# A fused attention and feed-forward block on one core: head loads and products by halves, late score and output folds in one batch

## The chip, the cores and the metric

The kernel runs on one core of one Trainium2 chip. A core has a matrix engine (TensorE, PE in the profile), a vector engine (VectorE, DVE), an activation engine (ScalarE, ACT), GpSimd (POOL), a queue engine for transfers (SyncE, SP) and 16 DMA engines. On-chip memory is SBUF, with 128 partitions; TensorE writes to PSUM. The metric is device time in microseconds.

## The reference

With x of 2048 tokens and 512 channels in bfloat16, and six vectors of 512 taken from a condition vector c:

```python
mod = (silu(c) @ w_mod).reshape(1, 6, 1, -1)      # sa, ca, ga, sb, cb, gb
h = layernorm(x) * (1 + ca) + sa
q, k, v = split(h @ wqkv)                          # 32 heads of 16 channels
logits = q . k[pos - 2*w] * 16**-0.5               # w = 0..7, positions below 0 masked
x = x + ga * ((softmax(logits) . v[pos - 2*w]) @ wo)
h = layernorm(x) * (1 + cb) + sb
x = x + gb * ((gelu(h @ w_gate) * (h @ w_up)) @ w_down)     # inner width 1792
```

So each token attends to eight tokens at distances 0, 2, ... 14.

## The kernel before

Tokens are cut into five groups, of 256, 256, 512, 512 and 512 (`GROUPS`). Each group passes through: the first layer norm and its shift and scale (`ln1`, then `transposed`, giving `hT`, channels on partitions), q, k and v (`emit_qkv`), attention and its projection (`emit_attention`), the second norm (giving `h2T`), and the feed-forward part (`emit_ffn`).

The head of the program: x's first 256 tokens are loaded, then `wm01`, the two blocks of w_mod that give sa and ca, then wq and wk. `mod_first` turns wm01 and silu(c) into columns with matrix products of one column (`modT_ps`): first for channel block 0, then for blocks 1 to 3. For group 0 VectorE applies shift and scale straight from PSUM (L561); `mod_keep` copies them to SBUF for the other groups, where ScalarE applies them (L519). The variance becomes 1/sqrt by a power on GpSimd (L513). Matmuls without use (`warm_ps`, L430) fill TensorE's time until the first data.

Attention works without gathers on k: VectorE multiplies q by shifted views of k, into product tiles `pq` of 128x2048 (L691). TensorE sums their channels with a 0/1 matrix of 32 columns, four such matmuls at once in four column groups (`LT`, L701: "fold"). For a 512-token group there are eight product tiles; two times four are made, and each four is folded by its own batch of 16 matmuls. Softmax runs over `LT` (`Lb`, `e`, `ss`). v goes through DRAM: `vT` is written to `scr`, and read back shifted as `vR`, four transfers of 32 partitions each for a tile (L667). VectorE forms `pv` = e times vR (L766, L772), TensorE folds these into `o_ps` (L782), also in two batches for a 512-token group, ScalarE copies them to `oT` (L788), and TensorE projects with wo (`x_ps`, L806).

The feed-forward part makes, for each 128-column unit of 1792, `g_ps` and `u_ps` (L847); ScalarE takes gelu and a copy (L856, L859), VectorE multiplies them into `hht` (L860), and TensorE forms `y_ps` (L873); VectorE adds it to x (L881), which is stored. gb is not applied at the end: `mod_row` makes gb as a row (`mb_ps`, L501, from the two halves of `wm5`), and VectorE scales w_down with it once (WdP, L901, seven instructions). ga is applied to wo in the same way, from wm2.

The order of everything is set ahead by a planner (`Plan.order`): each operation has an engine, an assumed duration, what it reads and writes, and a priority from the table `PRI`; the planner places them one after another, and each engine then runs its list in that order. Nearly all transfers are issued by SP in its planned order, and each issue can wait for the data it reads or the buffer that it overwrites.

Of the kernel before, what the change touches and what calls it, by code (L numbers as in the profile page):

```python
# [184 lines left out]
class Engines:  # L185
    def __init__(self, nc, pl):
        op = pl.op
        self.pe = lambda us, fn, **kw: op("pe", us, fn, **kw)
        self.act = lambda us, fn, **kw: op("act", us, fn, **kw)
        self.dve = lambda us, fn, **kw: op("dve", us, fn, **kw)  # L190
        self.pool = lambda us, fn, **kw: op("pool", us, fn, **kw)
        self.dma = lambda n, fn, bw=350e3, us=0.5, **kw: op("sp", us, fn, dma=n / bw, **kw)

# [5 lines left out]
BLOCKS2 = ()  # L199
PRI = {  # L200
        "ln1": (-1549, -553.9, -424.8, -117.9, 420.6),
        "qkv": (-226.2, 479.5, 310.9, 823.2, 1490.9),
        "att": (-63.2, 258.1, -1202.2, 1315.4, 916.4),
        "ffn": (1214.3, 2234.3, 2417.5, 2391, 546),
        "glu": (-1006.6, 100.6, -1510.2, -71.4, 1415.7),
        "mod": (393, -373, -33.5),
        "wo": 1028.5,
        "wd": 1181.4,
        "scr": -3561.5,
        "vR": -3846.6,  # L210
        "warm": (12, 4, 0, 3),
        "load": {"wv": -989.49, "x1": -989.99, "x2": -962.38, "wm2": -989.49, "wo": -888.99, "x3": -991.49,
        "wm3": -899.52, "wm4": -990.99, "x4": -981.04, "Wg": -864.95, "Wu": -877.79, "wm5": -867.98, "Wd":
        -873.85},
}
Plan.MARGIN = {"pe": 0.34, "act": 1.25, "dve": 0.46, "pool": -1.19, "sp": 1.04}
Plan.AHEAD = 2.79
Plan.SKEW = 1.27
# [4 lines left out]
def kernel(  # L223
# [40 lines left out]
    pool("trs", 8, space=bass.MemoryType.DRAM)  # L264
# [18 lines left out]
    onecol = ctile([P, 1], BF16, "onecol")  # L283
    M = ctile([P, H], BF16, "Mph")
# [24 lines left out]
    def consts_dve():  # L309
        nc.vector.memset(warm(), 0.0)  # L310
        nc.vector.memset(one1[:], 1.0)
        nc.vector.memset(neghalf[:], -0.5)
        nc.vector.memset(onecol[:], 1.0)

# [29 lines left out]
    dve(0.6, consts_dve, w=[(early, 0), one1, neghalf, onecol], pri=-1000)  # L344
# [26 lines left out]
    wm01 = T("vR", [P, 4, 2 * D], BF16, "wm01", "early")  # L371
# [21 lines left out]
    def load_rows(t, src, p, cuts, late=0.0):  # L393
        n = len(t.shape) and t.shape[1] // cuts
        for i in range(cuts):
            dma(1835e3 / cuts, lambda i=i: nc.sync.dma_start(
                out=t[:, i * n:(i + 1) * n, :],
                in_=src[i * n * P:(i + 1) * n * P, :].rearrange("(dt p) f -> p dt f", p=P)),
                w=[(t, k) for k in range(i * n, (i + 1) * n)], pri=p + 0.1 * i, bw=385e3)
# [3 lines left out]
    dma(1049e3, lambda: nc.sync.dma_start(out=wm01[:], in_=w_mod[:, 0:2 * D].rearrange("(t p) n -> p t n", p=P)),  # L403
        w=[wm01], pri=-999, bw=385e3)
    for b in range(3):
        dma(524e3, lambda b=b: nc.sync.dma_start(  # L406
            out=wqkv[b][:], in_=A_wqkv[:, b * D:(b + 1) * D].rearrange("(dt p) n -> p dt n", p=P)), w=[wqkv[b]],
            pri=(-998, -997, L["wv"])[b])
# [12 lines left out]
    load_rows(Wg, B_w_gate, L["Wg"], 2)  # L421
    load_rows(Wu, B_w_up, L["Wu"], 2)
    load_wm_halves(wm5, 5, L["wm5"])
    load_rows(WdP, B_w_down, L["Wd"], 2)
# [44 lines left out]
    def mod_first(src, p):  # L469
        parts = []  # L470
        for chs in ((0,), (1, 2, 3)):
            n = len(chs)
            mps = T("psF", [P, 2 * n], F32, "modT_ps")

            def cols(chs=chs, n=n, mps=mps):
                for half in range(2):
                    for i, ch in enumerate(chs):
                        col = mps[:, half * n + i:half * n + i + 1]
                        for kt in range(4):
                            nc.tensor.matmul(col, lhsT=src[:, kt, half * D + ch * P:half * D + (ch + 1) * P],  # L480
# [4 lines left out]
            pe(0.25 * n, cols, r=[src, scT, ident, onecol], w=[mps], pri=p)  # L485
# [3 lines left out]
    def mod_keep(parts, p):  # L489
        for lo, n, mps in parts:  # L490
            act(0.2, lambda lo=lo, n=n, mps=mps: nc.scalar.copy(out=scl[:, lo:lo + n], in_=mps[:, n:2 * n]), r=[mps],
                w=[(scl, 0)], pri=p)
            act(0.2, lambda lo=lo, n=n, mps=mps: nc.scalar.copy(out=modT[:, lo:lo + n], in_=mps[:, 0:n]), r=[mps],
# [13 lines left out]
    def norm(tok, xn, i, mean, rstd, p):  # L507
        dve(0.325, lambda: nc.vector.tensor_scalar(
            out=xn[:, i, :], in0=xrow(tok), scalar1=mean[:, i:i + 1], scalar2=rstd[:, i:i + 1], op0=ALU.subtract,
            op1=ALU.mult), r=[xkey(tok), mean, rstd], w=[(xn, i)], pri=p)  # L510
# [5 lines left out]
    tp0 = []  # L516

    def modulate(dst, src, dt, off, n, p, ins):
        act(act_us(n, 2), lambda: nc.scalar.activation(  # L519
            out=dst[:, dt, 0:n], in_=src(), func=ACT.Identity, scale=scl[:, off // 2 + dt:off // 2 + dt + 1],  # L520
            bias=modT[:, off + dt:off + dt + 1]), r=ins + [(scl, off), (modT, off)], w=[(dst, dt)], pri=p)

    def transposed_by_blocks(xns, dst, off, p):
        blk = T("blk" if off == 0 else "wq", [P, 16, P], BF16, "blk")
        trs = T("trs", [16, 32, 4, P], BF16, "trs", "t%d" % off)
        for half, xn in enumerate(xns):
            dve(1.14, lambda half=half, xn=xn: nc.vector.transpose(
                out=_ap(blk[:], [[32, 2], [P, 16], [1, 32]], offset=64 * half), in_=xn[:]), r=[xn], w=[(blk, half)],
                pri=p)
        for a in range(4):  # L530
            dma(131e3, lambda a=a: nc.sync.dma_start(
                out=bass.AP(trs.t.tensor, trs.t.offset + P * a, [[4 * P, 32], [32 * 4 * P, 16], [1, P]]),
                in_=blk[32 * a:32 * a + 32, :, :]), r=[blk], w=[(trs, a)], pri=PRI["scr"], bw=110e3)
        dma(524e3, lambda: nc.sync.dma_start(
            out=dst[:], in_=bass.AP(trs.t.tensor, trs.t.offset, [[4 * P, P], [P * 4 * P, DT], [1, SG]])),
            r=[trs], w=[(dst, dt) for dt in range(DT)], pri=PRI["scr"])
        for dt in range(DT):
            modulate(dst, lambda dt=dt: dst[:, dt, :], dt, off, SG, p, [(dst, dt)])

    def columns(t, dt, n, by_blocks):  # L540
        return _ap(t[:, dt, :], [[32, 4], [P, 4], [1, 32]]) if by_blocks else t[:, dt, 0:n]

    def transposed(xns, n, dst, off, p, seq, tags, split):
        per = 2 if n == SG else 4
        for dtp in range(DT // per):
            tp = T(tags[dtp], [P, per, n], BF16, "tp", seq)
            tp0.append(tp)
            for half, xn in enumerate(xns):
                def trans(half=half, dtp=dtp, tp=tp, xn=xn):
                    for i in range(2):  # L550
# [5 lines left out]
                pe(0.115 * per, trans, r=[xn, ident], w=[(tp, half)], pri=p)  # L556
            for dd in range(per):
                dt = per * dtp + dd
                if split:
                    lo, nm, mps = mod0[min(dt, 1)]  # L560
                    dve(0.07 + n * 1.041e-3, lambda dt=dt, dd=dd, tp=tp, i=dt - lo, nm=nm, mps=mps: nc.vector.tensor_scalar(  # L561
                        out=dst[:, dt, 0:n], in0=tp[:, dd, 0:n], scalar1=mps[:, nm + i:nm + i + 1],
                        scalar2=mps[:, i:i + 1], op0=ALU.mult, op1=ALU.add), r=[tp, mps], w=[(dst, dt)], pri=p)
                else:
                    modulate(dst, lambda dd=dd, tp=tp: tp[:, dd, 0:n], dt, off, n, p, [tp])

    def ln1(g, dst, p):
        xns = []
        tok0, n = GROUPS[g]
        for half in range(n // 256):  # L570
# [5 lines left out]
            xns.append(xn)  # L576
            for i in range(2):
# [4 lines left out]
            dve(0.09, lambda rstd=rstd, mv=mv: nc.vector.tensor_scalar_add(out=rstd[:], in0=mv[:, :, 1],  # L582
                                                                          scalar1=EPS), r=[mv], w=[rstd], pri=p)
            invsqrt(rstd, p)
            if g == 0:
                gp(2.4, consts_late, r=[ident, rstd], w=[NB, MA, MB], pri=-900)
            for i in range(2):
                norm(tok + P * i, xn, i, Mean(mv), rstd, p)
        if g in BLOCKS1:
            transposed_by_blocks(xns, dst, 0, p)  # L590
        else:
            transposed(xns, n, dst, 0, p, "ln1", ("psL",) if g == 0 else ("psF", "psF"), g == 0)

    class Mean(Tl):


        def __init__(self, mv):
            self.__dict__ = mv.__dict__

# [9 lines left out]
    def emit_qkv(g):  # L609
# [5 lines left out]
        if g == 0:  # L615
            for t in vs:
                gp(0.2, lambda t=t: nc.gpsimd.memset(t[:, :, 0:HALO], 0.0), w=[(t, "halo")], pri=-800)
        for step, (b, j) in enumerate(order):
# [3 lines left out]
            def mm(b, j, ps, jls, dts):  # L622
                for dt, jl in [(dt, jl) for dt in dts for jl in jls] if len(jls) == 1 or len(dts) == 1 else \
                        [(dt, jl) for jl in jls for dt in dts]:
                    lone = len(dts) == 1 and len(jls) > 1
                    nc.tensor.matmul(ps[:, jl, :], lhsT=wqkv[b][:, dt, j + jl:D:4], rhs=columns(hT[g], dt, n, g in BLOCKS1),  # L626
                                     start=(dt == 0 and (jl == 0 or not lone)),
                                     stop=(dt == DT - 1 and (jl == nj - 1 or not lone)))

            if g == 0 and step < 2:  # L630
                for k, dt in enumerate(range(DT)):
                    pe(2 * 0.115, lambda b=b, j=j, ps=ps, dt=dt: mm(b, j, ps, range(nj), (dt,)),
                       r=[wqkv[b], (hT[g], dt)], w=[ps], pri=p + 0.01 * k, pad=ps if dt == 0 else None)
# [23 lines left out]
    def emit_attention(g):  # L657
# [6 lines left out]
        for i, t in enumerate(vR[g]):  # L664
            rs = [(scr, (gg, i if GROUPS[gg][1] == SG else 0)) for gg in range(max(g - 1, 0), g + 1)]
            for r in range(4):
                dma(32 * 4 * njv * (n + 8) * 2, lambda r=r, t=t, i=i: nc.sync.dma_start(  # L667
# [5 lines left out]
                    r=rs, w=[(t, r)], pri=PRI["vR"] + 0.1 * g, bw=205e3)  # L673
# [263 lines left out]
```

## Time and profile before

| | us |
|---|---|
| median of 5 runs | 248.66 |
| range of the runs | 248.07 to 250.33 |
| the profiled execution | 250.68 |
| its span, first to last instruction | 248.5 |
| TensorE busy | 240.3 |
| VectorE busy | 159.2 |
| ScalarE busy | 159.7 |
| GpSimd busy | 17.3 |

The granted TensorE clock was 0.998 over the span. A time with an x behind it counts instructions. In a timeline line the columns are start, duration, engine, line of the kernel, operation, written tile and read tiles, shape, and in brackets the idle time ahead and what ended it. TensorE's instructions overlap, so a line's duration can exceed the distance to the next start.

### The profile page before, as it was taken

The numbers are of one execution on the slowest core, as the hardware profiler recorded it, in microseconds if no ns is written. First come the engines' busy times: TensorE is split into PE (matmuls) and PEld (weight loads), VectorE is DVE, ScalarE is ACT, GpSimd is POOL, SyncE is SP. The second block draws the span as 40 slices with busy tenths as digits, with TensorE's granted clock in tenths as the row PEclk, the third lists the DMA queues.
The fourth block names the chain that finished last, engine by engine and source line by source line (L and its number), as shares of the span: only waits on it lengthen the run. The fifth ranks groups of instructions, "written<-read, shape, count | busy, mean of one in ns | idle before, by whom it ended". The sixth has DMA issues, their size and how long they took to land.

```text
span 248.5 us, 4324 instructions
## 1 busy us (share of the span) xinstructions
PE 240.3 (97%) x1669; PEld 130.6 (53%) x1669; DVE 159.2 (64%) x303; ACT 159.7 (64%) x289; POOL 17.3 (7%) x39
## 2 busy tenths in 40 slices
PE   7899999997999999999999999999999999999994
PEld 3788655545864547575444445444454444444453
DVE  3689938978996499992799984299552221222222
ACT  2288989678729769488777488946679501666400
POOL 5334010010001000020000011000010000000000
PEclk9999999999999999999999999999999999999999
DMA  6999999999530119800119500001000000100011
GB/s 219 360 368 332 269 254 267 260 323 195 129 55 0 42 45 223 166 0 4 44 50 196 100 0 0 15 30 44 0 3 1 0 32 13 42 0 0 3 42 42
DMA packets 25398, 25.88 MB, mean 104 GB/s; under 512 B 1313, under 2 KB 23714, under 8 KB 25378
## 3 DMA queue, kind: packets, MB, share of 16 engines
q1 hardware_dynamic: 25376, 25.61, 39.9%
q8 instruction: 13, 0.21, 0.4%
q14 instruction: 7, 0.06, 0.1%
q10 hardware_dynamic: 2, 0.00, 0.0%
HBM read 21.40 MB, written 4.21 MB: 103 GB/s over the span
## 4 chain that ended last, share of the span: by engine, by line
PE 80%; DMA 9%; SPq 5%; ACT 4%; issue 1%; DVE 0%; ACTq 0%
PE g_ps L847 20%; PE u_ps L847 20%; PE y_ps L873 20%; PE qkv_ps L626 8%; DMA Wg<-in_B_w_gate_dram 5%; PE x_ps L806 5%; DMA wm<-in_w_mod_dram 4%; PE LT L701 3%; PE o_ps L782 3%; SPq L366 2%; PE tp L553 2%; SPq L389 1%; ACT hT L519 1%; ACT vT L647 1%; SPq L406 1%
## 5 line engine op out<-in xcount | busy, mean ns | idle before, releaser
L847 PE MATMUL g_ps<-h2T,Wg 128*128 128x512 bf16 (+1 forms) x280 | 57.9, 337 | 1.6 <-DMA Wg<-in_B_w_gate_dram 1.6
L847 PE MATMUL u_ps<-h2T,Wu 128*128 128x512 bf16 (+1 forms) x280 | 57.6, 337 | 0.0
L856 ACT ACTIVATE gl<-g_ps 128x512 bf16<-128x512 f32 x56 | 33.6, 600 | 28.1 <-PE g_ps L847 19.2
L873 PE MATMUL y_ps<-WdP,hht 128*128 128x512 bf16 (+1 forms) x238 | 50.4, 367 | 0.0
L860 DVE TENSOR_TENSOR hht<-gl,ub 128x512 bf16<-128x512 bf16 x56 | 23.3, 421 | 37.5 <-ACT ub L859 37.3
L859 ACT CAST ub<-u_ps 128x512 bf16<-128x512 f32 x56 | 32.9, 587 | 15.0 <-PE u_ps L847 15.0
L847 PEld LDWEIGHTS <-Wg 128*128 128x128 bf16 x280 | 26.7, 98 | 25.4 <-issue 2.8
L691 DVE TENSOR_TENSOR pq<-qT,kT 128x2048 bf16<-128x2048 bf16 x32 | 37.7, 1215 | 0.5 <-PE o_ps L782 0.5
L847 PEld LDWEIGHTS <-Wu 128*128 128x128 bf16 x280 | 27.0, 98 | 20.8 <-issue 1.1
L873 PEld LDWEIGHTS <-hht 128*128 128x128 bf16 x238 | 23.1, 98 | 25.0 <-issue 0.4
L766 DVE TENSOR_TENSOR pv<-e,vR 128x2048 bf16<-128x2048 bf16 x24 | 28.1, 1216 | 0.1
L881 DVE TENSOR_TENSOR x_sg<-y_ps,x_sg 128x512 bf16<-128x512 f32 (+1 forms) x17 | 10.5, 655 | 26.6 <-PE y_ps L873 26.6
L513 POOL TENSOR_TENSOR rstd<-rstd,neghalf 128x2 f32<-128x2 f32 x16 | 12.9, 813 | 165.0 <-DVE rstd L821 145.8
L626 PE MATMUL qkv_ps<-hT,wq 128*128 128x512 bf16 (+1 forms) x80 | 17.1, 337 | 0.5 <-DVE hT L561 0.3
L626 PE MATMUL qkv_ps<-hT,wk 128*128 128x512 bf16 (+1 forms) x80 | 16.7, 337 | 0.6 <-DMA wk<-in_A_wqkv_dram 0.4
L626 PE MATMUL qkv_ps<-hT,wv 128*128 128x512 bf16 (+1 forms) x80 | 15.5, 337 | 0.0
L806 PE MATMUL x_ps<-woP,oT 128*128 128x512 bf16 x64 | 15.3, 379 | 0.0
L813 ACT ACTIVATE xn<-x_sg 128x512 bf16<-128x512 bf16 x16 | 10.0, 630 | 6.3 <-DVE x_sg L810 6.1
L519 ACT ACTIVATE h2T<-tp,modT,scl 128x512 bf16<-128x512 bf16 (+1 forms) x20 | 12.3, 700 | 1.3 <-PE tp L553 1.3
L578 DVE BATCH_NORM_STATS2 st<-x_sg 128x6 f32<-128x512 bf16 x16 | 10.1, 680 | 3.3 <-DMA x_sg<-in_A_x_dram 3.3
L647 ACT CAST qT<-qkv_ps 128x512 bf16<-128x512 f32 x16 | 9.4, 597 | 3.6 <-PE qkv_ps L626 3.5
L810 DVE SCALAR_TENSOR_TENSOR x_sg<-x_ps,x_sg 128x512 bf16<-128x512 f32 x16 | 10.7, 683 | 1.4 <-PE x_ps L806 1.3
(89 smaller groups left out, 221.9 us busy)
## 6 DMA issues: line engine op xcount, KB each, us to landing
vR<-scr SPq DMA_DIRECT2D x24, 260.0 KB, 5.3
vR<-scr SPq DMA_DIRECT2D x8, 264.0 KB, 9.1
out_dram<-x_sg SPq DMA_DIRECT2D x15, 128.0 KB, 1.7
Wu<-in_B_w_up_dram SPq DMA_DIRECT2D x2, 896.0 KB, 10.2
scr<-vT SPq DMA_DIRECT2D x7, 256.0 KB, 6.7
WdP<-in_B_w_down_dram SPq DMA_DIRECT2D x2, 896.0 KB, 9.5
Wg<-in_B_w_gate_dram SPq DMA_DIRECT2D x2, 896.0 KB, 10.3
x_sg<-in_A_x_dram SPq DMA_DIRECT2D x3, 512.0 KB, 9.0
```

The source lines that it names most:

```text
L513: gp(0.75, lambda: nc.gpsimd.tensor_tensor(out=rstd[:], in0=rstd[:], in1=neghalf[:, 0:2], op=ALU.pow), r=[rstd, neghalf], w=[rstd], pri=p)
L519: act(act_us(n, 2), lambda: nc.scalar.activation(out=dst[:, dt, 0:n], in_=src(), func=ACT.Identity, scale=scl[:, off // 2 + dt:off // 2 + ...
L626: nc.tensor.matmul(ps[:, jl, :], lhsT=wqkv[b][:, dt, j + jl:D:4], rhs=columns(hT[g], dt, n, g in BLOCKS1), start=(dt == 0 and (jl == 0 or ...
L647: act(act_us(SG), lambda dst=dst, ps=ps: nc.scalar.copy(out=dst(), in_=ps[:]), r=[ps], w=w, pri=p)
L691: dve(1.145, lambda j=j, wg=wg, no=no, t=pq[m]: nc.vector.tensor_tensor(out=t[:], in0=_ap(q[g][:, j, :], [[0, no], [1, n]]), in1=_ap(kT[:, ...
L766: dve(1.145, lambda jj=jj, jl=jl, wg=wg, t=pv[m]: nc.vector.tensor_tensor(out=t[:], in0=_ap(e[:, wg, :], [[0, 4], [1, n]]), in1=vR[g][jj][ ...
L806: nc.tensor.matmul(x1_ps[:], lhsT=oT[:, j, c4 * P:(c4 + 1) * P], rhs=woP[:, j, :], start=(j == 0), stop=(j == 3))
L847: nc.tensor.matmul(ps[:, f, :], lhsT=Wt[:, dt, ft * P:(ft + 1) * P], rhs=columns(h2[g], dt, n, g in BLOCKS2), start=(dt == 0), stop=(dt == ...
L856: act(act_us(SG), lambda gl=gl, ps=gu[0]: nc.scalar.activation(out=gl[:], in_=flat(ps), func=ACT.Gelu_apprx_tanh), r=[gu[0]], w=[gl], pri= ...
L859: act(act_us(SG), lambda ub=ub, ps=gu[1]: nc.scalar.copy(out=ub[:], in_=flat(ps)), r=[gu[1]], w=[ub], pri=p)
L860: dve(0.339, lambda gl=gl, ub=ub, ht=hh[u // 2], u=u: nc.vector.tensor_tensor(out=ht[:, u % 2, :], in0=gl[:], in1=ub[:], op=ALU.mult), r=[ ...
L873: nc.tensor.matmul(y_ps[:], lhsT=hh[u // 2][:, u % 2, f * n + c4 * P:f * n + (c4 + 1) * P], rhs=WdP[:, ft, lo_d:hi_d], start=(ft == 0), st ...
```

## The change

- wm01 becomes two tiles, one for channels 0 to 255 and one for 256 to 511, each loaded by two transfers (sa's part and ca's part). `mod_first` works on these halves, the second behind the transposition of x.
- wq, wk and wv are each loaded in two transfers (row blocks 0-1 and 2-3), in the order x, wm01's first half, wq's first half, wm01's second half, wq's second half, x, wk, wv. Group 0 computes q, then k, then v; q by single row blocks, k and v by two.
- For groups 0 and 1 the 1/sqrt of the first norm is an Ln and an Exp on ScalarE (`rsqrt_act`), for group 0 token block by token block.
- For groups 3 and 4 (`MERGE`) all eight product tiles are made and then folded by one batch of 32 matmuls, for pq and for pv. Three of the eight tiles use the space of wq, wk and wv, and two of the output tiles use the PSUM of the score tiles.
- vR's four transfers are issued in the order 0, 2, 1, 3.
- Priorities and the planner's margins change, and so the order on every engine. Wg is now loaded right behind wo, then half of Wu, half of Wd, half of Wu, half of Wd, and wm5 last; mb_ps stands ahead of the first g_ps.
- Code for another way of transposing, which was switched off, is removed; a second queue for vR and a merged feed-forward part are added, both switched off (`SECOND`, `FMERGE`).

```diff
+LNACT = (0, 1)
+SECOND = ()
+MERGE = (3, 4)
+FMERGE = 0
...
+    def load_wm01(i):
+        for half in range(2):
+            lo = half * D + i * (D // 2)
+            dma(262e3, lambda half=half, lo=lo: nc.sync.dma_start(
+                out=wm01[i][:, :, half, :], in_=w_mod[:, lo:lo + D // 2].rearrange("(t p) n -> p t n", p=P)),
+                w=[(wm01[i], half)], pri=-999 + 0.5 * i + 0.1 * half, bw=385e3)
+
+    def load_wqkv(b, p):
+        for i in range(2):
+            dma(262e3, lambda i=i: nc.sync.dma_start(
+                out=wqkv[b][:, 2 * i:2 * i + 2, :],
+                in_=A_wqkv[2 * i * P:2 * (i + 1) * P, b * D:(b + 1) * D].rearrange("(o p) n -> p o n", o=2)),
+                w=[(wqkv[b], k) for k in range(2 * i, 2 * i + 2)], pri=p + 0.25 * i)
...
-        for chs in ((0,), (1, 2, 3)):
+        for i2, chs in enumerate(((0, 1), (2, 3))):
...
+    def rsqrt_act(out_, in_):
+        nc.scalar.activation(out=out_, in_=in_, func=ACT.Ln, bias=eps1[:])
+        nc.scalar.activation(out=out_, in_=out_, func=ACT.Exp, scale=-0.5)
...
+            if g == 0:
+                cut = ((0,), (1,), (2,), (3,)) if b == 0 else ((0, 1), (2, 3))
+                for k, dts in enumerate(cut):
+                    pe(0.23 * len(dts), lambda b=b, j=j, ps=ps, dts=dts: mm(b, j, ps, range(nj), dts),
+                       r=[(wqkv[b], dt) for dt in dts] + [(hT[g], dt) for dt in dts], w=[ps], pri=p + 0.01 * k)
...
-            for r in range(4):
-                dma(32 * 4 * njv * (n + 8) * 2, lambda r=r, t=t, i=i: nc.sync.dma_start(
+            for r in (0, 2, 1, 3):
+                queue, on = (nc.scalar, E.dma_act) if r in SECOND else (nc.sync, dma)
+                on(32 * 4 * njv * (n + 8) * 2, lambda r=r, t=t, i=i, queue=queue: queue.dma_start(
...
+        steps = 4 // njv
+        whole = g in MERGE
+        tags = ["prod"] * 8
+        if whole:
+            tags[5:] = "wq", "wk", "wv"
+
+        def products(name, jj):
+            at = 4 * jj if whole else 0
+            return [T(tags[at + m], [P, 8 // nb, n], BF16, name) for m in range(4)]
+
+        def joined(parts):
+            return [sum(parts, [])] if whole else parts
...
+        for jj, pq in enumerate(joined(pqs)):
             def fold(jj=jj, pq=pq):
-                for m in range(njv):
+                ms = len(pq) // (2 if n == SG else 1)
+                for m in range(ms):
...
-            pe(0.9, fold, r=pq + [M], w=LT, pri=p, pad=LT[0], cols=True)
+            pe(0.22 * len(pq), fold, r=pq + [M], w=LT, pri=base + jj, pad=LT[0], cols=True)
...
+        for jj, pv in enumerate(joined(pvs)):
+            o_ps = [T(("psB", "psB", "psL", "psL")[m], [P, nj, n], F32, "o_ps", "o" + "BBLL"[m]) for m in range(len(pv) // 2)]
```

## The prediction

> **What bounds the kernel now.** I read the page's busy shares first, then the 40 slices, the waits, TensorE's timeline around its longest idle stretch, the DMA rates in 2 us steps there, and last the chain.
>
> ```profile
> span 248.5 us, 4324 instructions
> PE 240.3 (97%) x1669; PEld 130.6 (53%) x1669; DVE 159.2 (64%) x303; ACT 159.7 (64%) x289; POOL 17.3 (7%) x39
> ...
> PE   7899999997999999999999999999999999999994
> ...
> DMA  6999999999530119800119500001000000100011
> ...
> PE g_ps L847 <- DMA Wg<-in_B_w_gate_dram: 1.6, 1, 1.6
> ```
>
> TensorE is busy 97% of the span; the DMA engines are full in slices 2 to 10 (to 60 us) and mostly idle later. So there are two stages: up to 60 us loads can set the pace, after that TensorE alone.
>
> ```profile
> 50.53 0.59 PE L501 MATMUL mb_ps<-wm,wide 128*128 128x512 bf16 x2
> 51.71 0.59 PE L501 MATMUL mb_ps<-wm,wide 128*128 128x512 bf16 x2 [0.58 <-DMA wm<-in_w_mod_dram]
> ...
> 57.34 0.38 PE L847 MATMUL g_ps<-h2T,Wg 128*128 128x256 bf16 x2
> 59.36 0.83 PE L847 MATMUL g_ps<-h2T,Wg 128*128 128x256 bf16 x6 [1.64 <-DMA Wg<-in_B_w_gate_dram]
> ```
>
> TensorE reaches the first feed-forward product at 57.34, does two matmuls, and stands until the second half of Wg lands at 59.3. From 60 to 245 us it is busy 185.0 of 185.0. The chain agrees:
>
> ```profile
> 46.86 12.46 DMA Wg<-in_B_w_gate_dram
> ...
> 139.76 0.98 PE LT L701 x16
> 140.74 0.97 PE g_ps L847 x4
> 141.71 0.86 PE u_ps L847 x4
> ...
> 233.24 12.14 PE y_ps L873 x70
> ```
>
> The last matmul ends at 233.24 + 12.14 = 245.4, and 3.1 us (add, store, end) follow. So span = landing 59.36 + TensorE's work behind it 186.0 + 3.1 = 248.5. The profiled execution took 250.68, 2.2 more than its span; the median 248.66 lies 2.0 below that time. I add 0.2 to a span for a median.
>
> The head's own stalls (0.27, 0.44, 0.53 us) lie ahead of a wait for Wg, so they cost nothing today.
>
> **What the new order does at that point.** In before, Wg's halves are the last loads of this stage; the last half of wm5 (the rows for gb) was issued at 45.56 and served at 51.71. In after, Wg comes right behind woP, and the last loads are the second half of WdP and then both halves of wm5. TensorE's program puts mb_ps (gb's row, four matmuls) directly ahead of the first g_ps. So TensorE still stands once, now at mb_ps's third matmul, with all feed-forward work behind it. The transfers ahead of the last one are the same set: x 2.1 MB, w_mod 3.1, wqkv 1.6, wo 0.5, three feed-forward weights 5.5, scr of groups 0 to 2 1.1, vR of groups 0 and 1 2.1: 16.1 MB.
>
> **Work behind the landing.** Before: 186.0. Now also behind it: the last two mb_ps matmuls (0.43, where all four were done before), the two g_ps done before (0.22), and four 512-column k matmuls of the last group that the order puts later (0.86): +1.5. Away: for groups 3 and 4 the score tiles and the output tiles are folded in one batch of 32 column-tiled matmuls, not two of 16. The chain rows price a batch: 16 of 512 columns in four column groups should stream like four full ones, 0.86; they take 0.98, and the block behind them 0.97 instead of 0.86: 0.23 a batch. Four batches fewer: -0.9. Sum 186.0 + 1.5 - 0.9 = 186.6. A merged fold waits for eight products; it stands in TensorE's order where the second half stood, behind feed-forward blocks that cover the wait. If a cover fails, it costs one product, 1.2 us (L691's row), per batch; I take 0, since the last pq of group 3 ended near 109.3 where the fold began at 110.6.
>
> Break-even follows: after is faster only if its last load lands 0.6 us before 59.36.
>
> **Where wm5 lands.** This decides, and no row shows it.
>
> ```profile
> 50.00:52.00 2.00, 1.42 (x8) 0.58 (x6) 1.26 (x5) 1.27 (x4) 0.69 (x1) 1.00 1.05 420
> 52.00:54.00 2.00, 2.00 (x11) 1.03 (x10) 1.53 (x4) 1.38 (x3) 0.00 (x0) 1.00 1.06 329
> 54.00:56.00 2.00, 2.00 (x18) 1.32 (x16) 2.00 (x5) 2.00 (x5) 0.00 (x0) 1.00 1.06 202
> 56.00:58.00 2.00, 1.72 (x9) 0.76 (x7) 1.37 (x4) 1.97 (x6) 0.00 (x0) 1.00 1.12 171
> ```
>
> The last column is GB/s. Summed over the span, 16.1 MB had moved by 54.0, but Wg's second half (0.92 MB) landed only at 59.3: a tail of 5.3 us in which vR of group 2, queued behind it, moved. Lower bound: no tail, 54.0. Upper: the whole tail, 59.3. wm5's half has 0.26 MB, and the half of it issued at 45.56 landed 6.1 us later, Wg's half issued at 46.87 took 12.5. I take the middle, 56.7, nearer neither row.
>
> *Packets.* wm01 was one load in 2 KB rows; it is now four in 512 B rows. The rate of 4 to 6 us, 386 GB/s over 16 engines, is 85 ns a packet: 32 per engine, 2.7 us. The trace has no 512 B load from HBM to 128 partitions. The nearest row in size is vR of the first groups, 528 B at 187 GB/s between 28 and 34 us: 45 to 49 ns a packet; 128 per engine would take 5.8 to 6.3 us, up to +3.6. [...] So 56.7 + 0.4 = 57.1.
>
> *vR's order.* Its four tiles of 32 partitions are now issued 0, 2, 1, 3. The rows: 187, 183 and 203 GB/s while vR moves, 361 and 420 while weights of 128 partitions do. [...]
>
> **The head, costed at nothing.** Six more DMA issues (0.45 to 0.5 us each on SP): the wk and wv halves and x queue behind them, 3 us, with five or more loads in flight. The first rstd: one DVE add (0.17) and a POOL power (0.71) become Ln and Exp on ScalarE (four of some 0.17) behind a table load (1.28) that starts once silu is done. c_ps moves ahead of seven warm-up matmuls. Matmuls of q, k, v by halves are the same 48. Cover for all: TensorE's wait at mb_ps. Without it, I estimate TensorE there at 57.34 - 0.58 (old wait) - 1.73 (mb_ps and four k matmuls now later) = 55.0, less some 0.3 in the head: 54.7. Two table loads fewer (9, not 11) take 2.6 us from ScalarE, which is no bound. WdP's scaling (7 x 0.683 = 4.8 us on VectorE) ran at 53 to 57 and now waits for gb: it falls in the stretch 60 to 80, 17.7 of 20 busy. There y_ps waits for it. But VectorE does pv of group 1 and two pq (7 us) while TensorE waits at mb_ps, so I take 0, at most 2.5.
>
> **Sum.** 57.1 + 186.6 + 3.1 = 246.8 span, 247.0 median: -0.7%.
>
> **Rivals.**
> (B) The tail is a matter of bytes and of vR behind, not of the last load's size: wm5 lands at 59.3 as Wg did. 59.3 + 186.6 + 3.1 = 249.0, median 249.2; no difference to be measured. For it: same set of bytes, DMA share above 1 throughout. Against: small loads landed sooner.
> (C, the other side) 512 B packets cost what vR's cost: 56.7 + 3.6 = 60.3, median 250.2, slower. Place: wm01, the second load; it shifts all that follows in a full queue. It decides from a landing of 60.0, some 46 ns a packet. For it: the row of 528 B. [...]
> [...]
>
> **How the numbers follow.** A 0.52 (own range 245.8 to 247.9), B 0.18, C 0.13, D 0.17. What measurement can tell from no change is about 0.5%, 1.2 us: faster is below 247.4. Nearly three quarters of A and all of D lie there: 0.54. Same: the rest of A and most of B, 0.29. Slower: C and a little of B, 0.17. The range leaves out half of D and of C: 244.8 to 249.8.
>
> **What would show it.** TensorE's longest idle stretch stands at mb_ps, ended by wm, at about 57; none at g_ps. LT and o_ps of the last two groups appear as x32, with 0.98 + 0.86 us. Behind the landing TensorE idles under 0.5 us. GB/s in the slices where wm01 moves stays above 330. The prediction is wrong if that wait ends after 58.7 or before 55.5, or if TensorE idles again between 75 and 82 us for WdP or near 110 and 150 us for a merged fold.

## The result, and the profile after

The changed kernel takes 248.77 us (median of 44 executions, 247.12 to 252.37), the kernel before in the same rounds 249.06 (79 executions, 247.84 to 255.48). The ratio is 0.9985, 95% interval 0.997 to 1.000: no difference that this measurement can tell. The prediction had 247.0, faster by 0.7%. Medians here are of all executions, while ratios leave out disturbed ones, so the two differ where times spread widely (most in the variant with vR's order undone, below: 252.25 over 18 executions, 250.62 over the 11 that its ratio counts).

The profiled execution of the changed kernel took 249.97. Its page, answering the lines shown of before:

```profile
span 247.9 us, 4316 instructions
...
PE 239.8 (97%) x1666; PEld 131.4 (53%) x1666; DVE 158.8 (64%) x302; ACT 158.6 (64%) x293; POOL 17.8 (7%) x37
...
PE   7799989998999999999999999999999999999995
...
PEclk9799999999999999999999999999999999999999
DMA  5999999998700019700108700001000000100011
```

TensorE is as busy as before, and the DMA engines are still full up to 60 us. New is the second slice: TensorE at 7 tenths, with a clock of 7 tenths. TensorE's timeline has the long stall where it was forecast, at the third mb_ps matmul, and none at g_ps:

```profile
55.76 1.03 PE L646 MATMUL qkv_ps<-hT,wq 128*128 128x512 bf16 x4
57.19 0.59 PE L523 MATMUL mb_ps<-wm,wide 128*128 128x512 bf16 x2 [0.40 <-DMA wm<-in_w_mod_dram]
58.46 0.59 PE L523 MATMUL mb_ps<-wm,wide 128*128 128x512 bf16 x2 [0.68 <-DMA wm<-in_w_mod_dram]
58.89 1.03 PE L888 MATMUL g_ps<-h2T,Wg 128*128 128x256 bf16 x8
```

The waits there sum to 1.1 us, where before had 0.58 and 1.64. The chain says the same: the last load, then TensorE to the end, with the merged folds as x32.

```profile
48.20 1.88 SPq L396
50.12 8.29 DMA wm<-in_w_mod_dram
...
110.11 1.84 PE LT L740 x32
...
232.82 12.14 PE y_ps L914 x70
```

From 60 to 245 us TensorE is busy 184.94 of 185.00. So the end is 189.4 us (247.9 - 58.46) behind the start of that third matmul. The question is what sets that start, and why a late start in a profile says little about the median.

### The profile page after: what moved, and what is told of

The parts are those of the page before. It is cut to its first block, busy times and chain, and to the rows that moved or that the text cites. A ratio compares the mean times of both kernels' runs of the same rounds, so it can differ in the third digit from the quotient of the medians.

```text
span 247.9 us, 4316 instructions
## 1 busy us (share of the span) xinstructions
PE 239.8 (97%) x1666; PEld 131.4 (53%) x1666; DVE 158.8 (64%) x302; ACT 158.6 (64%) x293; POOL 17.8 (7%) x37
## 4 chain that ended last, share of the span: by engine, by line
PE 83%; DMA 8%; ACT 4%; SPq 2%; DVE 1%; issue 0%
PE u_ps L888 20%; PE g_ps L888 20%; PE y_ps L914 20%; PE qkv_ps L646 10%; DMA wm<-in_w_mod_dram 5%; PE x_ps L850 5%; PE o_ps L825 3%; DMA vR<-scr 2%; PE LT L740 2%; ACT hT L546 2%; PE tp L560 2%; ACT kT L668 1%; ACT qT L668 1%; SPq L396 1%; PE LT L770 1%; PE ss L785 1%
## 5 line engine op out<-in xcount | busy, mean ns | idle before, releaser
L914 PE MATMUL y_ps<-WdP,hht 128*128 128x512 bf16 (+1 forms) x238 | 51.2, 367 | 0.0
L888 PEld LDWEIGHTS <-Wg 128*128 128x128 bf16 x280 | 27.2, 98 | 21.4 <-issue 0.4
L536 POOL TENSOR_TENSOR rstd<-rstd,neghalf 128x2 f32<-128x2 f32 x14 | 13.5, 966 | 169.7 <-DVE rstd L865 109.2
L646 PE MATMUL qkv_ps<-hT,wq 128*128 128x512 bf16 (+1 forms) x80 | 17.9, 358 | 0.0
L546 ACT ACTIVATE h2T<-tp,modT,scl 128x512 bf16<-128x512 bf16 (+1 forms) x20 | 12.8, 695 | 2.2 <-PE tp L560 2.2
L857 ACT ACTIVATE xn<-x_sg 128x512 bf16<-128x512 bf16 x16 | 10.1, 630 | 4.8 <-DVE x_sg L854 4.5
L668 ACT CAST kT<-qkv_ps 128x512 bf16<-128x512 f32 x16 | 9.4, 589 | 4.6 <-PE qkv_ps L646 4.5
## 6 DMA issues: line engine op xcount, KB each, us to landing
vR<-scr SPq DMA_DIRECT2D x8, 264.0 KB, 10.1
```

Source lines behind the costliest of these rows:

```text
L536: gp(0.75, lambda: nc.gpsimd.tensor_tensor(out=rstd[:], in0=rstd[:], in1=neghalf[:, 0:2], op=ALU.pow), r=[rstd, neghalf], w=[rstd], pri=p)
L546: act(act_us(n, 2), lambda: nc.scalar.activation(out=dst[:, dt, lo:lo + n], in_=src(), func=ACT.Identity, scale=scl[:, off // 2 + dt:off / ...
L668: act(act_us(SG), lambda dst=dst, ps=ps: nc.scalar.copy(out=dst(), in_=ps[:]), r=[ps], w=w, pri=p)
L888: nc.tensor.matmul(ps[:, f, :], lhsT=Wt[:, dt, ft * P:(ft + 1) * P], rhs=h2[g][:, dt, 0:n], start=(dt == 0), stop=(dt == DT - 1))
L914: nc.tensor.matmul(y_ps[:], lhsT=hh[u // 2][:, u % 2, f * n + c4 * P:f * n + (c4 + 1) * P], rhs=WdP[:, ft, lo_d:hi_d], start=(ft == 0), st ...
```

## The experiments

"Changed" is the changed kernel. For the variants of it the order of every engine was kept and one thing moved, unless said otherwise. Ratios are to the kernel before, run in the same rounds. None of the kernels leaves work out.

### What the wait at mb_ps is worth

First, the two wm5 loads ahead of the second half of WdP:

```diff
 SP: scr x2
+SP: wm5 first half, wm5 second half
 SP: WdP second half
-SP: wm5 first half, wm5 second half
```

> The changed kernel, with the two wm5 loads issued ahead of the second half of WdP instead of behind it; nothing else moves on any engine. Theory 1 (the landing of the last load ahead of mb_ps decides until TensorE's own arrival does): 0.92 MB less ahead of wm5, it lands before TensorE comes to mb_ps at 56.8; the waits of 0.40 and 0.68 us there go, and the time falls by that sum, 1.1 us, to about 247.7, no more. Theory 2 (what follows in the queue shares the engines, so the order of the last loads makes no difference): wm5 lands at 58 or later, the time stays within 0.4 us of the changed kernel.

247.91 (247.57 to 248.92), ratio 0.9961 (0.9943 to 0.998). Second, mb_ps behind the first two pairs of g_ps and u_ps:

```diff
-PE: mb_ps, g_ps, u_ps, g_ps, u_ps
+PE: g_ps, u_ps, g_ps, u_ps, mb_ps
```

> The changed kernel, with mb_ps (and ScalarE's copy of it) behind the first two pairs of g_ps and u_ps instead of ahead of them; the loads are as they were. Theory 1: TensorE comes to the first g_ps at 56.8 with Wg and Wu in place and does not stop; wm5's landing at 58.4 is covered by 3.5 us of matmuls; the time falls by the two waits, 1.1 us, to about 247.7. If TensorE's late arrival is what set the time instead and the two waits are only slack that some later wait takes up (rival), it stays at 248.8.

247.97 (247.33 to 249.25), ratio 0.9969 (0.9946 to 0.9991). In both the stall is gone, and TensorE's timeline of the first shows its own arrival:

```profile
55.35 1.03 PE L646 MATMUL qkv_ps<-hT,wq 128*128 128x512 bf16 x4
56.21 1.03 PE L523 MATMUL mb_ps<-wm,wide 128*128 128x512 bf16 x4
57.07 1.04 PE L888 MATMUL g_ps<-h2T,Wg 128*128 128x256 bf16 x8
```

Two ways of taking the wait away give gains that cannot be told apart: 0.8 to 0.9 us between medians, 0.4 to 0.6 us by the ratios (0.9961 and 0.9969 against the changed kernel's 0.9985, from other rounds; the intervals overlap). The profile's waits summed to 1.1. Both narrow the spread, from 5.2 us to 1.4 and 1.9. In the first wm5 lands 4.3 us after its issue, in the changed kernel 8.6. So the landing of wm5 is on the path, and the narrower spread says that much of the scatter of the changed kernel's times is its scatter; but the gain ends where TensorE arrives, at 56.2.

### Why the head is late

In the changed kernel's profile the first q product starts at 9.06, in that of before at 8.32; then TensorE's clock halves:

```profile
8.03 0.35 PE L502 MATMUL modT_ps<-scT,wm 128*128 128x1 bf16 x8 [0.60 <-DMA wm<-in_w_mod_dram]
8.77 0.26 PE L502 MATMUL modT_ps<-scT,wm 128*128 128x1 bf16 x4 [0.39 <-DMA wm<-in_w_mod_dram]
...
9.06 2.73 PE L646 MATMUL qkv_ps<-hT,wq 128*128 128x256 bf16 x12
```

By stretch (last three columns: granted clock, DMA share, GB/s):

```profile
8.00:10.00 2.00, 1.58 (x23) 1.24 (x24) 0.96 (x3) 0.22 (x2) 0.00 (x0) 0.65 1.09 378
10.00:12.00 2.00, 2.00 (x11) 1.35 (x10) 1.50 (x4) 0.23 (x2) 0.00 (x0) 0.50 1.08 355
```

My first theory was the clock. Useless matmuls were put into those waits:

```diff
-                    for i in range(n):
+                    for i in (range(n), i2 and warm_mm(3 - half))[0]:
```

> The changed kernel, with five useless 512-column matmuls (warm_ps) put into TensorE's waits for wm01's second tile: three behind the transposition of x, two between the two halves. Nothing else moves. Theory 1 (the head is on the path): the granted clock of 8 to 12 us stays near 1.00 instead of 0.65 and 0.50, the twelve first q matmuls take some 1.4 us instead of 2.7, and v, scr and so the queue of loads come about 1 us earlier: TensorE arrives at mb_ps at about 55.6 instead of 56.8, wm5 lands about 0.5 to 1 us earlier than 58.4; median 0.7 to 1.2 us below the changed kernel, about 247.8. Theory 2 (the tail is a matter of bytes): wm5 lands at 58.4 all the same, TensorE only waits longer at mb_ps; same time, 248.8.

249.30, ratio 1.0003 (0.9979 to 1.0026). The clock did stay at 1.00 in the profile and the twelve matmuls took 1.48, yet the first q product began at 9.20 and wk then came 0.51 late: what the clock gave back, the next load took.

```profile
9.20 1.48 PE L646 MATMUL qkv_ps<-hT,wq 128*128 128x256 bf16 x12
11.19 0.63 PE L646 MATMUL qkv_ps<-hT,wk 128*128 128x256 bf16 x4 [0.51 <-DMA wk<-in_A_wqkv_dram]
```

So curing the dip alone gains nothing that can be measured. Nor do these waits always bring it. The kernel with mb_ps late has the same head and the same waits, and its clock stays at 1.00:

```profile
8.14 0.35 PE L502 MATMUL modT_ps<-scT,wm 128*128 128x1 bf16 x8 [0.60 <-DMA wm<-in_w_mod_dram]
8.89 0.25 PE L502 MATMUL modT_ps<-scT,wm 128*128 128x1 bf16 x4 [0.40 <-DMA wm<-in_w_mod_dram]
...
9.16 1.48 PE L646 MATMUL qkv_ps<-hT,wq 128*128 128x256 bf16 x12
```

Of the seven profiles of kernels with this head and nothing put into the waits, only the first shows the dip. What decides between the two was not found.

Then the load itself. wm01 in one tile again, one transfer with rows of 2 KB (issued once, where the first of the four stood), everything else as changed:

```diff
-                out=wm01[i][:, :, half, :], in_=w_mod[:, lo:lo + D // 2].rearrange("(t p) n -> p t n", p=P)),
+                out=wm01[0][:], in_=w_mod[:, 0:2 * D].rearrange("(t p) (h n) -> p t h n", p=P, h=2)),
```

> The changed kernel, with wm01 in one tile and loaded by one transfer in 2 KB rows, where the first of its four stood; the other three are not issued. The products by halves, q, k and v by halves and all orders stay. Theory 1 (wm01's small rows and its wq half in between make the head late): modT_ps no longer waits between the halves, first q matmul at 8.4 or earlier instead of 9.1, v and with it the queue of loads 0.8 to 1.3 us earlier, wm5 landing as much earlier: 247.6 to 248.0. Theory 2 (the last landing is set by the sum of bytes): the head is earlier all the same, but wm5 lands at 57.5 to 58.4 as before and the time stays at 248.8.

247.13 (246.69 to 251.05), ratio 0.9918 (0.9898 to 0.9938): 1.7 us below the changed kernel's ratio, and more than the expected 0.8 to 1.2. The first q product starts at 8.43 at full clock, with no wait for wk, and the first store of v to scr is issued 1.9 us earlier. This kernel's lines, and then the changed kernel's:

```profile
8.43 1.47 PE L646 MATMUL qkv_ps<-hT,wq 128*128 128x256 bf16 x12
...
16.13 0.64 SPq L672 DMA_DIRECT2D scr<-vT  x1
```

```profile
18.07 0.63 SPq L672 DMA_DIRECT2D scr<-vT  x1
```

Here one profile stands for the others: the three profiles of kernels with one transfer issue scr at 16.1 to 16.6, the eight with the changed head (the filled waits included) at 17.4 to 18.2. With mb_ps late as well:

> As the one before, and mb_ps behind the first two pairs of g_ps and u_ps, so that wm5's landing is covered: the time shows TensorE's own arrival alone. Theory 1: against the kernel with mb_ps late alone (247.9) it gains the head's shift, 0.8 to 1.3 us: 246.6 to 247.1. If the head's lateness is made up elsewhere before 56 us (at LT's wait for Lb, 0.6 to 1.2 us near 33), it gains under 0.4: 247.5 or more.

246.81 (six executions, 246.62 to 250.59), ratio 0.9899 (0.9863 to 0.9935), the fastest of the study and better than both kernels. TensorE, with nothing to wait for, arrives at 54.68:

```profile
53.81 1.03 PE L646 MATMUL qkv_ps<-hT,wq 128*128 128x512 bf16 x4
54.68 1.04 PE L888 MATMUL g_ps<-h2T,Wg 128*128 128x256 bf16 x8
```

One transfer differs from the four in number, in rows, and in that all of wm01 now comes ahead of wq. Is it the 512 B rows or the four transfers? wm01 of the kernel before by four transfers, by columns and by rows:

```diff
-    dma(1049e3, ... out=wm01[:], in_=w_mod[:, 0:2 * D] ...)
+    for i in range(4):
+        dma(262e3, ... out=wm01[:, :, i * 256:(i + 1) * 256], in_=w_mod[:, i * 256:(i + 1) * 256] ...)
...
+    for i in range(4):
+        dma(262e3, ... out=wm01[:, i, :], in_=w_mod[i * P:(i + 1) * P, 0:2 * D])
```

> The kernel before, with wm01 loaded by four transfers of 256 columns (rows of 512 B) instead of one (rows of 2 KB); to be read against its pair with four transfers of 2 KB rows. Theory 1 (the packets cost): while wm01 moves, the rate falls to some 180 GB/s, as in the changed kernel between 4.4 and 5.6 us, wm01 is complete some 2 us later than in the pair, and the first q matmul and all loads behind shift by 1 to 2 us; the time rises by 0.5 to 2 us over the pair's, since Wg's landing decides there. Rival (the number of transfers and SP's 0.5 us for each cost, not the packets): both kernels of the pair are late alike, by up to 1.5 us, and differ by less than 0.3 us.

> The kernel before, with wm01 loaded by four transfers of 128 rows of 2 KB each instead of one. Theory 1: above 350 GB/s while wm01 moves, wm01 complete within 0.7 us of the kernel before; time within 0.5 us of it. Rival (the issues cost): wm01 late by 1.5 us, the time up by as much, as in the pair.

512 B rows: 250.91, ratio 1.0054 (1.0026 to 1.0083). 2 KB rows: 250.40, ratio 1.0036 (1.0012 to 1.0060). So four transfers with rows of 2 KB already cost 0.9 us of the whole time, by the ratio; what the small rows add is not resolved (the intervals overlap). The first q product, at 9.55 and 9.06, settles nothing: in the four profiles of the kernel before, head unchanged, it starts at 8.32, 8.56, 8.91 and 9.67. The rate is steadier, and tells both parts apart. Before, one transfer:

```profile
3.20:3.60 0.40, 0.40 (x2) 0.15 (x1) 0.00 (x0) 0.00 (x0) 0.26 (x3) 1.00 0.43 123
...
4.00:4.40 0.40, 0.40 (x2) 0.15 (x1) 0.40 (x2) 0.00 (x0) 0.00 (x0) 1.00 1.05 410
4.40:4.80 0.40, 0.40 (x3) 0.15 (x1) 0.40 (x1) 0.00 (x0) 0.00 (x0) 1.00 1.05 410
...
5.60:8.00 2.40, 2.40 (x42) 1.59 (x41) 1.33 (x4) 0.17 (x1) 2.10 (x8) 1.00 1.05 375
```

Four transfers with rows of 2 KB:

```profile
4.00:4.40 0.40, 0.40 (x2) 0.15 (x1) 0.40 (x2) 0.00 (x0) 0.00 (x0) 1.00 0.86 148
4.40:4.80 0.40, 0.40 (x3) 0.15 (x1) 0.40 (x2) 0.00 (x0) 0.00 (x0) 1.00 0.98 159
...
5.60:8.00 2.40, 2.40 (x21) 1.10 (x20) 1.16 (x3) 0.17 (x1) 2.13 (x7) 1.00 1.05 381
```

The changed kernel, four with rows of 512 B:

```profile
4.00:4.40 0.40, 0.40 (x2) 0.15 (x1) 0.40 (x2) 0.40 (x1) 0.33 (x2) 1.00 0.36 101
4.40:4.80 0.40, 0.40 (x2) 0.15 (x1) 0.40 (x1) 0.40 (x1) 0.33 (x3) 1.00 0.74 177
...
5.60:8.00 2.40, 1.55 (x29) 1.05 (x26) 1.36 (x4) 0.59 (x3) 0.01 (x1) 1.00 1.09 341
```

With one transfer there is one dip of 0.4 us, to 123 GB/s; with four, in these two profiles, the rate stays between 101 and 230 GB/s for 1.2 us from 4.0 us on, whatever the rows. Over the whole stretch, in every profile:

| wm01 | profiles | GB/s, mean of 2 to 8 us |
|---|---|---|
| one transfer, rows of 2 KB | 8 | 338 to 347 |
| four, rows of 2 KB | 2 (the last of this section's tests is one) | 298 and 304 |
| four, rows of 512 B | 9 | 265 to 292 |

An estimate from this table: 6 us at some 41 GB/s less are 0.25 MB, or 0.7 us at the 375 GB/s of before; the rows cost a further 27 GB/s, 0.4 us. The rows' own rate shows best at 6.0 to 6.4 us, where wm01 moves alone, by estimate: 0.93 and 1.07 MB had moved by 6.0, of the 1.31 that x's first part and wm01 have, and wq is issued behind them. First 512 B, then 2 KB:

```profile
6.00:6.40 0.40, 0.40 (x2) 0.00 (x0) 0.31 (x1) 0.00 (x0) 0.31 (x3) 1.00 1.08 326
```

```profile
6.00:6.40 0.40, 0.40 (x2) 0.00 (x0) 0.31 (x1) 0.00 (x0) 0.31 (x3) 1.00 1.04 387
```

That is, by estimate from these rates, 25 ns for a packet of 512 B on each of 16 engines, and 19% more time for the same bytes. The last test puts four transfers with 2 KB rows into the changed kernel:

```diff
-                out=wm01[i][:, :, half, :], in_=w_mod[:, lo:lo + D // 2] ...
+                out=wm01[0][:, 2 * i + half, :, :], in_=w_mod[(2 * i + half) * P:(2 * i + half + 1) * P, 0:2 * D] ...
```

> The changed kernel with wm01 in one tile as in the run with one transfer, but loaded by four transfers of 128 rows of 2 KB, issued where the four of the changed kernel stood. Theory 1 (four transfers cost, whatever their rows): the rate of 3.6 to 5.6 us falls to 150 to 250 GB/s as in the kernel before with four such loads, first q matmul at 9.0, time 248.2 to 248.7. Theory 2 (the rows of 512 B cost): above 350 GB/s from 4 us on, first q matmul at 8.5, 247.1 to 247.5.

249.51, ratio 1.0009 (0.9986 to 1.0032): outside both expectations, not better than with 512 B rows, 2.3 us above one transfer. But more than the rows differs here. The first product of modT_ps needs all four transfers, and wq's first half moves ahead of the last two, so TensorE waits 0.83 and 0.48 and q starts at 9.78; in the profile the twelve q matmuls take 2.62 us (1.47 with one transfer) with a clock of 8 tenths in the second slice (6.2 to 12.4 us), and 19 of 22 executions show a mean clock below 0.997. So this test says that 2 KB rows alone do not cure the head; it puts no price on the rows. The number of transfers is the larger part by the kernel before and by the rates. Why the rate falls with four in place of one was not found.

### vR's order

Undone in the changed kernel, and made alone in the kernel before:

```diff
-            for r in (0, 2, 1, 3):
+            for r in (0, 1, 2, 3):
```

> The changed kernel, with vR's four transfers issued in the order 0, 1, 2, 3 again; nothing else moves. Theory 1: the new order lets vR of the first groups move some 8 per cent faster (about 200 GB/s where the kernel before shows 175 to 190), worth up to 0.5 us of landing before mb_ps: undone, the time rises by 0.2 to 0.6 us, with wm5 landing at 58.6 to 59. Rival: the rate in those stretches differs for other reasons (which load follows vR); same time within 0.2 us, and the same rate of 200 GB/s where vR moves.

> The kernel before, with vR's four transfers issued in the order 0, 2, 1, 3; nothing else changes. Theory 1 (the order is worth what its undoing cost the changed kernel, about 1.9 us of landing): the wait at g_ps goes or shrinks, the time falls to where TensorE arrives by itself, 247.8 to 248.0, with a narrow spread. Rival (the order matters only in the changed queue): same time, 248.7 to 249.4, and 170 to 210 GB/s where vR moves, as before.

Undone: 252.25 (249.05 to 254.09), ratio 1.0082 (1.0051 to 1.0114), some 2.4 us worse than the changed kernel's ratio, where 0.2 to 0.6 had been expected. Alone on the kernel before: 248.36, ratio 0.997 (0.9948 to 0.9991), 0.7 us and less than expected (247.8 to 248.0), and in the profile no wait at g_ps, which TensorE reaches at 57.13. So the order is worth over 2 us in the changed kernel, and in the kernel before no more than the wait that is there. There vR of the first group takes 7.9 us in this one profile (median of four transfers, issue to landing), against 8.9, 9.4, 9.1 and 9.1 in the four profiles of that kernel. In the changed kernel the first profile without the order (249.67, a quick one) showed no such difference, so two more were taken:

> The changed kernel with vR in the order 0, 1, 2, 3, profiled once more, since its first profile (249.67) stands below its median and shows vR no slower than with the other order. Theory 1 (the order delays the landing): in an execution of 250 to 252.5 the third mb_ps matmul begins at the time less 2.1 and less 189.4, at 58.7 to 61, and the transfers of vR take longer from issue to landing than the 10.0 and 10.5 us of the changed kernel. Rival: the landing is at 58.2 again and the time lies elsewhere.

> As the one before: theory 1 puts the third mb_ps matmul at the execution's time less 191.5, with vR's transfers slower from issue to landing; the rival puts the excess elsewhere.

251.13 and 253.90. In the first the start of the third mb_ps matmul is where the theory put it (251.13 - 191.5 = 59.63):

```profile
58.39 0.59 PE L523 MATMUL mb_ps<-wm,wide 128*128 128x512 bf16 x2 [0.82 <-DMA wm<-in_w_mod_dram]
59.61 0.59 PE L523 MATMUL mb_ps<-wm,wide 128*128 128x512 bf16 x2 [0.62 <-DMA wm<-in_w_mod_dram]
```

In the second it is not (62.4 expected):

```profile
59.16 0.59 PE L523 MATMUL mb_ps<-wm,wide 128*128 128x512 bf16 x2 [2.30 <-DMA wm<-in_w_mod_dram]
60.72 0.95 PE L523 MATMUL mb_ps<-wm,wide 128*128 128x512 bf16 x2 [0.96 <-DMA wm<-in_w_mod_dram]
```

The rest, 1.7 us, lies behind the landing: the granted clock is 0.93 from 54 to 62 us, which hold the 3.3 us of waits, and 0.86 from 62 to 70, up to 1.7 us of lost clock by estimate. In this execution a lower clock stands beside the late landing; that the waits bring it was not shown. vR of these two takes 10.1 to 10.8 us, the changed kernel's 10.0 and 10.5 in its first profile, 8.8 and 9.2 in its second: the difference lies within what one kernel's executions scatter, so through which transfers the order acts is open in the changed kernel.

### The merged folds

The fastest kernel without MERGE; the planner places groups 3 and 4 anew, the order up to mid-span is the same:

```diff
-MERGE = (3, 4)
+MERGE = ()
```

> The kernel with one transfer for wm01 and mb_ps late (246.8), without the merged folds of groups 3 and 4, which the planner then places as two batches of 16 each; up to the middle of the span the order is the same. Theory 1: four more batches at 0.23 us each on an engine that never stops behind 55 us: slower by 0.9 us, 247.7. Rival: the switch of the column groups costs nothing behind 512-column matmuls, or the merge brings waits for the eighth product that cost as much: within 0.3 us of 246.8.

247.98 against 246.81, ratio 0.9961 (0.9933 to 0.9989). From the first g_ps to the end of the span it takes 191.0 us (246.1 - 55.10), with the merge 189.9 (244.6 - 54.68): the merge, with the order that the planner makes of it, is worth 1.1 us. (The two ratios' intervals just touch: the merged kernel has six executions.) The folds of these groups, first with and then without:

```profile
L740 PE MATMUL LT<-pq,Mph 128*32 128x512 bf16 x96 | 5.9, 381 | 0.0
L825 PE MATMUL o_ps<-pv,F 128*32 128x512 bf16 x96 | 5.9, 381 | 0.1
```

```profile
L825 PE MATMUL o_ps<-pv,F 128*32 128x512 bf16 x96 | 6.4, 382 | 0.0
L740 PE MATMUL LT<-pq,Mph 128*32 128x512 bf16 x96 | 6.3, 382 | 0.0
```

0.9 us of it is in the folds' own busy time.

### Is the profile of before a typical execution?

It took 250.68, 2.0 above the median of its runs. The kernel before was profiled three times more, the changed kernel once more:

> The kernel before, unchanged, profiled once more, since its first profiled execution (250.68) stands 2.0 us above the median. Theory 1 (the runs differ by when Wg's second half lands): an execution of 248 to 249 shows the wait at g_ps shorter by what it is faster, with the landing at 57 to 58 instead of 59.36, and 186 us of work behind it all the same. Rival: the landing is at 59.3 again and the two microseconds lie elsewhere, in the clock or behind the landing.

> The kernel before, unchanged, profiled a third time. If this execution takes 248 to 249, theory 1 puts the end of TensorE's wait for Wg (or its own arrival) at 56.8 to 57.8, since 189.1 us lie between that wait's end and the end of the span in both profiles so far; the rival puts it at 59.4 with less than 188 us behind.

> The kernel before, unchanged, profiled a fourth time; as for the third: the end of the wait at the execution's time less 2.15 and less 189.1, whatever that time is.

> The changed kernel, unchanged, profiled once more. Theory 1: the third mb_ps matmul begins at the execution's time less 2.1 and less 189.4; in an execution near the median of 248.7 that is 57.2, against 58.46 in the first profile (249.97).

| kernel, execution | wait ends | span | span less wait's end | time less span |
|---|---|---|---|---|
| before, 250.68 | 59.36 | 248.5 | 189.1 | 2.2 |
| before, 250.91 | 59.58 | 248.7 | 189.1 | 2.2 |
| before, 250.12 | 58.77 | 247.9 | 189.1 | 2.2 |
| before, 251.30 | 59.98 | 249.1 | 189.1 | 2.2 |
| changed, 249.97 | 58.46 | 247.9 | 189.4 | 2.1 |
| changed, 247.87 | no wait, 56.38 | 245.8 | 189.4 | 2.1 |

In the last row TensorE does not stand; 56.38 is the start of the third of these four mb_ps matmuls, two of 0.215 us behind the first:

```profile
55.95 1.03 PE L523 MATMUL mb_ps<-wm,wide 128*128 128x512 bf16 x4
```

The quickest of before's, as TensorE's timeline has it:

```profile
57.17 0.38 PE L847 MATMUL g_ps<-h2T,Wg 128*128 128x256 bf16 x2
58.77 0.83 PE L847 MATMUL g_ps<-h2T,Wg 128*128 128x256 bf16 x6 [1.21 <-DMA Wg<-in_B_w_gate_dram]
```

Each execution is the end of one wait, plus 189.1 or 189.4, plus 2.1 or 2.2; only the first of these varies. All four profiles of before are later than its median: 249.06 less 2.2 and 189.1 puts the end of the wait at 57.8 in a median execution, 1.6 us earlier than in the profile that the prediction read. And 57.8 leaves next to no wait: without one, TensorE would start that third g_ps matmul two matmuls (0.22 us) behind its arrival, at 57.4 to 58.1 in these four profiles. So in a median execution of before TensorE hardly stands for Wg at all. That step is worked out, not seen: no profile of before near its median came up. Of the kernel's 79 executions 18 took 250.12 or longer, and all four profiles did; whether taking a profile itself delays these loads is open.

## Why the prediction was wrong

**The failed step: "I add 0.2 to a span for a median."** A span lies 2.0 to 2.3 below its own execution's time in every run. The 0.2 came from setting the profile's span (248.5) beside a median (248.66) of other executions, and so took the 2.0 us between 250.68 and 248.66 for something outside the span. It was inside: Wg had landed late. With the right constant the prediction's own sum, 57.1 + 186.6 + 3.1 = 246.8, gives 248.9, and 248.77 was measured. The same step made the gain: 57.1 was held against a landing of 59.36, while the median execution has 57.8. The break-even ("0.6 us before 59.36") lay at 57.2 for a median, so the forecast landing was hardly a gain at all: the wait that the change was to shorten is nearly absent from a median execution.

**Work behind the landing: right.** 186.6 + 3.1 = 189.7 forecast, 189.4 measured (before 189.1). The merge saves 1.1, not 0.9. WdP's scaling and the waits for eight products cost nothing, as taken.

**Landing 57.1: right by luck.** The changed kernel's median puts it at 57.3 (248.77 - 2.1 - 189.4). But 56.7 was the middle of a bracket read from an execution whose last load was late, and two terms that the sum has at nothing nearly cancel. "The head, costed at nothing" costs 1.7 us (number, rows and place of wm01's transfers together). Its cover, the wait at mb_ps, is not a cover: SP issues in its planned order, scr waits for v, and every later load stands behind it. In the changed kernel's profile scr is issued at 18.07, woP behind it at 18.75, wm5 from 48.20 on, and its second half ends TensorE's wait at 58.46; with one wm01 transfer scr is issued at 16.13, woP at 16.82 and wm5 from 45.77 on, and the four mb_ps matmuls run from 54.95 to 56.28. (In the second profile of the changed kernel scr is issued at 17.40, and the third mb_ps matmul starts at 56.38 without a wait.) So a late head makes the last landing late too. And vR's order, for which the sum has no term, is worth some 2 us. vR of the first group in the kernel before went from about 9.1 to 7.9 us, 13%, in one profile with the new order, and the whole time fell by 0.7 us.

**Packets: the choice was right, the question incomplete.** The +0.4 in 56.7 + 0.4 = 57.1 was the author's assumption, set against the +3.6 of vR's row, and no run shows it. What the runs showed in its place are rates: they put the rows at 0.4 us over 2 to 8 us by estimate, and where such rows move alone, 326 GB/s stand against 387, 19% more time. What was not asked is what four transfers cost instead of one: with rows of 2 KB 0.7 us by the rates and 0.9 us of the whole time in the kernel before. The prediction counted six more issues by SP's time, not by the rate that they leave.

**Uncovered arrival 54.7: right for a head that is not late.** Without waits and with one wm01 transfer TensorE arrived at 54.68. With the change's own head it is 55.9 to 56.8.

**Rivals.** D, with 0.17, stood for a landing ahead of TensorE's own arrival at 54.7, by vR's order: the order does count (over 2 us in the changed kernel), but TensorE arrives at 55.9 to 56.8 with this head, so 245.0 is not reachable. B's outcome, no difference to be measured, came true, but not by its mechanism: wm5 landed 0.9 us sooner than Wg had in its profile, and issued ahead of WdP's half it landed in half the time. C is refuted: its sign came (the rate while wm01 moves did not stay above 330 GB/s), but the rate fell with 2 KB rows as well, and a packet of 512 B took 25 ns, not 46.

## What to carry to other kernels

Before a sum is made from a profile, ask whether that execution is a typical one: where its time stands in the spread of the runs, and which single wait makes the difference. A gain counted from a wait that varies from run to run must be counted against that wait's usual size. And where later loads stand behind an early store in one in-order queue, as here behind scr, the head is not free: with scr issued 1.9 us later, wm5 was issued 2.4 us later (18.07 against 16.13, 48.20 against 45.77), so the stall at the end of the stage does not hide it.

## What the runs showed of the hardware

- Four transfers of 256 KB in place of one of 1 MB at the start of the kernel: 298 and 304 GB/s over 2 to 8 us with rows of 2 KB, 265 to 292 with rows of 512 B, against 338 to 347 (19 profiles). In the two profiles shown the rate is 101 to 230 GB/s for 1.2 us from 4.0 us on.
- Rows of 512 B, moving alone by estimate: 326 GB/s from 6.0 to 6.4 us in one profile, or 25 ns a packet on each of 16 engines; rows of 2 KB: 387 in another.
- A clock of 0.50 from 10 to 12 us followed waits of 0.60 and 0.39 us between one-column matmuls in one profile; after waits of 0.60 and 0.40 in another the clock stayed at 1.00. With waits of 2.30 and 0.96 us in a third profile it was 0.93 from 54 to 62 us and 0.86 from 62 to 70. What sets it was not shown.
- With the order 0, 2, 1, 3 of four transfers to 32 partitions each, the first vR of the kernel before takes 7.9 us from issue to landing in one profile, against 8.9 to 9.4 in four with the order 0, 1, 2, 3; the whole time falls by 0.3%.
